# Attention prepared one step earlier, the first MLP's raw weights loaded ahead into their final places, and their low parts on VectorE

## The chip, the cores and the metric

The kernel runs on one core of one Trainium2 chip. The metric is the device time of one execution in microseconds (us). Times are compared between executions on the same chip.

## The reference

Four inputs of attention per batch and head: 512 local and 32 global tokens, 4 batches, 8 heads, head size 64. A local query sees the 32 global keys and the local keys within 32 positions; a global query sees all keys. The result, 2176 rows of 512, goes through two MLPs.

```python
def sm(s):
    e = np.exp(s - np.max(s, axis=-1, keepdims=True))
    return e / (np.sum(e, axis=-1, keepdims=True) + 1e-09)
out_g = np.matmul(sm(scale * q_g @ k_all.T), v_all)              # k_all: global and local keys
s_l = concat([scale * q_l @ k_g.T, where(|i - j| <= 32, scale * q_l @ k_l.T, -1e9)])
out_l = np.matmul(sm(s_l), concat([v_g, v_l]))
x = [out_g, out_l] as rows of 512                                # 2176 x 512
h = x @ moe_w_in;   x = np.maximum(0.01 * h, h) @ moe_w_out      # 512 x 2048, 2048 x 512
h = x @ moe2_w_in;  x = (h - np.tanh(h)) @ moe2_w_out
```

The four weight matrices come as 64-bit floats.

## The kernel before

**Numbers.** Matmuls of the MLPs and of the scores are made of three: each operand is split into a rounded high part and a low part (value minus high part), and high x high, low x high and high x low are added in PSUM. ScalarE writes the high part, VectorE or GpSimd subtracts.

**Weights.** A weight tile is 128 x 512. `load_w` (line 99) brings its 64-bit words (512 KB) into a raw buffer, of which there are two (tag `wraw`). `convert_w` (113) makes 32-bit floats of them: an Abs on ScalarE (119) and four VectorE steps (120, 121, 125, 128), of which the last reads the raw buffer for the last time. `split_w` (133) then writes the high part on ScalarE (134) and subtracts the low part (135), for the first MLP on GpSimd. The 16 tiles of the first layer (`in`) stay in `win_h` and `win_l`; those of the second (`out`) are kept in few buffers and stored to DRAM, from where later chunks fetch them (`wo_fetch`). `w_jobs` (656) lists the conversions in order, in and out in turn; `w_load` issues the next load, `w_job` converts the tile loaded longest ago. The conversion steps may not be put ahead of the last attention output (`issue_after`, 684).

**Attention.** There are 32 units (pairs of heads for half a sequence). The work on unit pp is: `k_prep` and `q_prep` (transposes, then high and low parts, 321, 322, 334, 335), `score` (three matmul groups), `smax_a` (mask and row minimum on VectorE, 374; exponential on ScalarE, 380), `smax_b` (sums, reciprocals, and the normalisation, on GpSimd for units under 16, line 394, else on VectorE, 399), `p_trans` (transposes of the probabilities, two copies on ScalarE, 412), `av` (products with the values, high and low part, 437, 439), `g_score` (the global queries' scores). `stage(pp)` (742) lists, in TensorE's order: score and softmax of pp, keys and queries of pp+1, the transposes and then the value products of pp-1, the global scores of pp. Steps of the global rows (`gtodo`) are put in between.

**Order.** A prologue runs stages 0 to 8 (`PRE`, line 51) and converts three first-layer tiles (`LW`). Then come 80 items of the first MLP, (chunk c, tile f) for five chunks of 512, 512, 512, 256 and 384 rows: `mlp1_a` is the first layer for tile f, `mlp1_b`, two items later (`SKEW`), adds the second layer's product. Beside the items of chunks 0 to 2 run the remaining stages (`beside`, 840), eight beside the 16 items of chunk 0. In chunk 0 each item also converts one `in` and one `out` tile (869 to 872). The second MLP's weights are converted into DRAM beside items 22 to 44 (`w2_job`), then 80 items of the second MLP follow. TensorE's instructions up to item 77 stand in program order by hand (`fix`, 799); on the other engines a planner orders instructions by priority and its own costs; SP issues all DMAs in order.

**PSUM.** The eight banks are `h`, four `y` and three `att` banks; in the prologue the attention uses `att` and `y` in turn, later only the three `att` banks (`tag`, 737).

The functions that the diff touches, and what calls them:

Of the kernel before, what the change touches and what calls it, by code (L numbers as in the profile page):

```python
# [13 lines left out]
I32 = mybir.dt.int32  # L14
# [7 lines left out]
def kernel(  # L22
# [28 lines left out]
    PRE, LW, SKEW = 9, 3, 2  # L51
# [17 lines left out]
    win_h = [persist.tile([128, ND, 128], F32R, name=f"winh{f}") for f in range(NF)]  # L69
    win_l = [persist.tile([128, ND, 128], F32R, name=f"winl{f}") for f in range(NF)]  # L70
# [120 lines left out]
    def mlp1_g(c, f, h):  # L191
# [165 lines left out]
    def norm(pp):  # L357
        return "pool" if pp < 16 else "dve"
# [44 lines left out]
    def p_trans(pp, h, tag):  # L403
# [7 lines left out]
        pt = att.tile([128, 2, 2, 128], F32, tag="pt", name="pt", bufs=4)  # L411
        nc.scalar.activation(pt.rearrange("p j c q -> p (j c q)"), ps, AF.Copy)
# [143 lines left out]
    def w2_place(kind, f, t):  # L556
        if kind == "in":
            split_w(t, flat(win_h[f]), flat(win_l[f]), nc.vector)
# [97 lines left out]
    w_jobs = []  # L656
    for f in range(LW):
        w_jobs.append(("in", f))
    for f in range(NF):
        if f:  # L660
            w_jobs.append(("out", f - 1))
        if f + LW < NF:
            w_jobs.append(("in", f + LW))
    w_jobs.append(("out", NF - 1))
    w_jobs.reverse()
    w_raw = []
# [5 lines left out]


    def w_load():
        if w_jobs:
            kind, f = w_jobs.pop()
            w_raw.append((kind, f, load_w(kind, w1_in if kind == "in" else w1_out, f)))

    def w_job():
        if not w_raw:  # L680
            return
        kind, f, raw = w_raw.pop(0)
        after = anchor[0] if 1 & 2 and anchor[0] is not None else last_av[0] if 1 & 1 else None
        with tc.issue_after(after.ins) if after is not None and nw[0] >= 0 else ExitStack():
            w = convert_w(raw)
        if kind == "in":
            split_w(w, flat(win_h[f]), flat(win_l[f]), nc.gpsimd)
        else:
            wo_split(f, w)
# [6 lines left out]
            later.append(store)  # L696

# [31 lines left out]
    jobs_done = [0]  # L729
# [12 lines left out]
    def stage(pp):  # L742
# [3 lines left out]
        if pp < NU // 2:  # L746
            ops.append(lambda: (score(pp, [tag(), tag()]), smax_a(pp), smax_b(pp)))
        nx = pp + 1
        if nx < NU // 2:
            if pp % 2:  # L750
                ops.append(lambda: load_kq((pp + 3) // 2))
            ops.append(lambda: (k_prep(nx, tag()), q_prep(nx, tag())))
            if nx % (2 * NP) == 0:
                ops.append(lambda: qg_prep(nx // (2 * NP), tag()))
        if pp > 0:
            ops.append(lambda: p_trans(pp - 1, 0, tag()))
            ops.append(lambda: (gtodo.pop(0)() if gtodo else None, p_trans(pp - 1, 1, tag())))

            def values_of():
                av(pp - 1, tag())  # L760
                if pp < NU // 2:
                    g_score(pp, tag())
                if gtodo:
                    gtodo.pop(0)()
                if pp % 2 == 0:
                    load_v((pp + 2) // 2)

            ops.append(values_of)
        else:
            ops.append(lambda: g_score(pp, tag()))  # L770
        hv, p = divmod(pp, NP)
        b, a = divmod(hv, 2)
        if pp < NU // 2 and a == 1 and p % 2 == 1:
            quad = p // 2

            def put():
                gtodo.extend([
                    lambda: (g_load(b, 2 * quad), g_smax(b, quad)),
                    lambda: (g_trans(b, quad, tag()), g_trans2(b, quad, tag())),
                    lambda: (g_av(b, quad, 0, tag()), g_load(b, 2 * quad + 1)),  # L780
                    lambda: g_av(b, quad, 1, tag()),
                ])

            ops.append(put)
# [22 lines left out]
    if True:  # L807
# [8 lines left out]
        w_load()  # L816
        qg_load(0)
        load_v(0)
        load_kq(1)
# [4 lines left out]
        w_load()  # L824
        for pp in range(PRE):
            for op in stage(pp):
                op()
            if pp >= 3 and jobs_done[0] < LW:
                w_job()
                w_load()  # L830
                stores()
                jobs_done[0] += 1
# [131 lines left out]
```

## Time and profile before

| | |
|---|---|
| median of 3 runs | 1006.79 us (1005.72 to 1009.12) |
| profiled execution, own time | 1006.56 us |
| its span, first to last instruction | 1004.8 us |
| TensorE busy, mean granted clock | 939.9 us (94%), 0.971 |
| VectorE, ScalarE, GpSimd busy | 663.6, 544.2, 102.0 us |
| data moved | 127.13 MB, mean 127 GB/s |

All rows are of the one profiled execution, and microseconds count from its first instruction. PE is TensorE's matmul, DVE is VectorE, ACT ScalarE, POOL GpSimd, SP the engine that issues the DMAs. Instructions that follow each other on an engine overlap a little at their ends, so a sum of durations is more than the busy time. A TensorE that is busy may still run at half clock: PEclk is the granted share of 2.4 GHz.

### The profile page before, as it was taken

Reading aid. Unit: us, or ns where it says so; the run is one execution under the profiler, and the core shown is the slowest. Engines: PE = TensorE matmul, PEld = TensorE weight load, DVE = VectorE, ACT = ScalarE, POOL = GpSimd, SP = SyncE. Lnnn points to the kernel's source line nnn. Section 1 sums busy time; section 2 is a strip of 40 time slices with the busy share of each in tenths; the row PEclk is TensorE's granted clock in tenths of the full one; section 3 lists DMA queues with packets and bytes.
Section 4 is the critical chain, followed back from the end, with each engine's and each line's share of the span. In section 5 each row is a group of like instructions: output and inputs, shape, how many; then the busy total and the mean of one; then the engine's idle time right before and its main releaser. Section 6 shows DMA issues by size and latency. Waiting matters only on the chain.

```text
span 1004.8 us, 15724 instructions
## 1 busy us (share of the span) xinstructions
PE 939.9 (94%) x5480; PEld 785.6 (78%) x5480; DVE 663.6 (66%) x1489; ACT 544.2 (54%) x1231; POOL 102.0 (10%) x123
## 2 busy tenths in 40 slices
PE   4877988889999999998999999999999999999998
PEld 3655766667787787786789999888888888899987
DVE  2456978864356675765421333988888888888886
ACT  4566655654555455554532344755554655655565
POOL 3334343421000000000000000000000000000022
PEclk9779999899999999998999999999999999999999
DMA  7345666675547779875565677200200010010010
GB/s 161 87 109 146 192 188 182 178 220 162 152 134 228 224 230 268 249 236 179 157 220 183 192 216 230 95 1 1 74 1 1 21 43 1 1 43 1 1 33 22
DMA packets 144943, 127.13 MB, mean 127 GB/s; under 512 B 89184, under 2 KB 107616, under 8 KB 144864
## 3 DMA queue, kind: packets, MB, share of 16 engines
q1 hardware_dynamic: 144864, 126.13, 42.1%
q8 instruction: 43, 0.70, 0.3%
q14 instruction: 36, 0.29, 0.1%
HBM read 100.40 MB, written 25.69 MB: 125 GB/s over the span
## 4 chain that ended last, share of the span: by engine, by line
PE 65%; DMA 15%; DVE 9%; ACT 6%; issue 2%; SPq 2%; ACTq 0%; DVEq 0%
PE h L55 29%; PE o L55 19%; PE y L55 11%; DMA wraw<-in_moe_w_in_dram 4%; DMA wraw<-in_moe_w_out_dram 3%; DMA w2od<-wf 2%; DMA wf<-w2od 2%; ACT e L380 2%; DVE wf L128 2%; PE avps L55 2%; DVE wt L125 2%; ACT wf L119 2%; PE sps L55 1%; DVE wf L120 1%; PE ptps L410 1%
## 5 line engine op out<-in xcount | busy, mean ns | idle before, releaser
L55 PE MATMUL h<-xh,winh 128*128 128x512 f32 (+2 forms) x640 | 236.3, 369 | 3.1 <-ACT g L196 3.0
L55 PE MATMUL h<-xl,winh 128*128 128x512 f32 (+2 forms) x640 | 231.6, 362 | 0.0
L55 PE MATMUL h<-xh,winl 128*128 128x512 f32 (+2 forms) x640 | 231.5, 362 | 0.0
L55 PEld LDWEIGHTS h<-xh,winh 128*128 128x128 f32 x640 | 122.0, 191 | 20.8 <-ACT g L196 3.9
L55 PEld LDWEIGHTS h<-xl,winh 128*128 128x128 f32 x640 | 121.8, 190 | 16.7
L55 PEld LDWEIGHTS h<-xh,winl 128*128 128x128 f32 x640 | 122.0, 191 | 15.7
L55 PE MATMUL y<-gh,woh 128*128 128x512 f32 (+2 forms) x320 | 123.2, 385 | 0.2 <-ACT yst L225 0.2
L55 PE MATMUL y<-gh,wol 128*128 128x512 f32 (+2 forms) x320 | 116.8, 365 | 0.0
L55 PE MATMUL y<-gl,woh 128*128 128x512 f32 (+2 forms) x320 | 116.5, 367 | 0.0
L55 PE MATMUL o<-wo2h,gh 128*128 128x512 f32 x255 | 100.2, 393 | 0.0
L55 PE MATMUL o<-wo2l,gh 128*128 128x512 f32 x255 | 99.5, 390 | 0.0
L55 PE MATMUL o<-wo2h,gl 128*128 128x512 f32 x255 | 98.2, 392 | 0.0
L592 ACT ACTIVATE u<-h 128x512 f32<-128x512 f32 (+2 forms) x80 | 42.6, 532 | 94.9 <-PE h L55 72.2
L198 DVE TENSOR_TENSOR gl<-g,gh 128x512 fp32r<-128x512 f32 (+2 forms) x80 | 51.7, 646 | 63.6 <-ACT gh L197 63.5
L380 ACT ACTIVATE e<-e,st 128x224 f32<-128x224 f32 (+1 forms) x128 | 58.7, 460 | 34.0 <-DVE st L374 33.6
L119 ACT ACTIVATE wf<-wraw 128x512 f32<-128x512 f32 x64 | 42.6, 666 | 62.8 <-DMA wraw<-in_moe_w_in_dram 21.2
L196 ACT ACTIVATE g<-h 128x512 f32<-128x512 f32 (+2 forms) x80 | 42.2, 527 | 58.0 <-PE h L55 56.8
L618 POOL TENSOR_TENSOR gl<-p,gh 128x256 fp32r<-128x256 f32 x16 | 11.9, 742 | 558.9 <-ACT gh L617 557.0
L55 PEld LDWEIGHTS y<-gl,woh 128*128 128x128 f32 x320 | 61.3, 192 | 8.7
L617 ACT ACTIVATE gh<-p 128x512 fp32r<-128x512 f32 (+2 forms) x80 | 45.5, 568 | 41.1 <-DVE p L601 41.1
L120 DVE TENSOR_SCALAR wf<-wf 128x512 f32<-128x512 f32 x64 | 31.8, 502 | 54.1 <-ACT wf L119 53.9
L55 PEld LDWEIGHTS y<-gh,woh 128*128 128x128 f32 x320 | 61.4, 192 | 7.7 <-ACT yst L225 0.4
(112 smaller groups left out, 1752.6 us busy)
## 6 DMA issues: line engine op xcount, KB each, us to landing
wraw<-in_moe_w_in_dram SPq DMA_DIRECT2D x32, 512.0 KB, 4.6
wraw<-in_moe_w_out_dram SPq DMA_DIRECT2D x32, 512.0 KB, 4.1
woh<-wod SPq DMA_DIRECT2D x64, 256.0 KB, 3.8
wol<-wod SPq DMA_DIRECT2D x64, 256.0 KB, 3.2
qr<-in_q_l_dram SPq DMA_DIRECT2D x32, 128.0 KB, 3.3
vn<-in_v_l_dram SPq DMA_DIRECT2D x32, 128.0 KB, 2.8
wod<-woh SPq DMA_DIRECT2D x16, 256.0 KB, 4.0
wod<-wol SPq DMA_DIRECT2D x16, 256.0 KB, 3.3
```

Of the source, the lines that this page charges most:

```text
L55: nc.tensor.matmul(o, lhsT, rhs, start=start, stop=stop)
L119: nc.scalar.activation(w, hw.bitcast(F32), AF.Abs)
L120: nc.vector.tensor_scalar_max(w, w, TINY)
L125: nc.vector.scalar_tensor_tensor(out=t, in0=hw, scalar=-0x40000000, in1=t, op0=ALU.bitwise_and, op1=ALU.bitwise_or)
L128: nc.vector.scalar_tensor_tensor(out=w.bitcast(I32), in0=lw, scalar=29, in1=t, op0=ALU.logical_shift_right, op1=ALU.bitwise_or)
L196: anchor[0] = nc.scalar.activation(g[:, :N], h[:, :N], AF.Prelu, alpha=0.01)
L198: nc.vector.tensor_sub(gl[:, :N], g[:, :N], f32(gh)[:, :N])
L380: nc.scalar.activation(e[:, h, j, s0 : s0 + n], e[:, h, j, s0 : s0 + n], AF.Exp, bias=st[:, k : k + 1], scale=-1.0, accum_out=st[:, 4 + k ...
L410: nc.tensor.transpose(ps[:, k * 128 : (k + 1) * 128], e[:, h, j, c0 : c0 + 128], ident)
L592: nc.scalar.activation(u, h, AF.Square)
L617: nc.scalar.activation(gh[:, :N], p, AF.Copy)
L618: eng["pool" if i == order2[-1] and [0, 16][0] <= f < [0, 16][1] else "dve"].tensor_sub(gl[:, :N], p, f32(gh)[:, :N])
```

## The change

One more stage runs in the prologue. In a stage, keys and queries of the next unit are now prepared ahead of the unit's score, and the value products of unit s-2 open the stage; the transposes of unit s-1 close it. All 16 raw tiles of the first layer are loaded in the prologue, each into the memory that its two parts take in the end (one tile of 128 x 2 x 512 for both, tag `win{f}`); one conversion follows each stage from the third on, eight in all. The other eight are converted beside items 0 to 7 of chunk 0. Second-layer tiles alone use the two raw buffers, and their next load is issued right behind a conversion. The low parts of all first-MLP weights go to VectorE. GpSimd normalises units 0 to 7 only; for these, the second copy of the transposed probabilities goes from ScalarE to VectorE. The probabilities have two buffers instead of four, the values of the global rows two instead of one. The second MLP's conversions may now not be put ahead of the activation's low part (before: of the activation).

```diff
-    PRE, LW, SKEW = 9, 3, 2
+    PRE, SKEW = 10, 2
+    win_h, win_l = {}, {}
+    def win_tile(f):
+        t = persist.tile([128, 2, DM], F32R, tag=f"win{f}", name=f"win{f}")
+        win_h[f], win_l[f] = [t[:, k].rearrange("p (k n) -> p k n", k=ND) for k in range(2)]
+        return t
...
-    def load_w(kind, w, f):
-        raw = mlp.tile([128, DM, 2], I32, tag="wraw", name="wraw", bufs=2)
+    def load_w(kind, w, f, raw=None):
+        if raw is None:
+            raw = mlp.tile([128, DM, 2], I32, tag="wraw", name="wraw", bufs=2)
...
-        split_w(w, hi, lo, nc.gpsimd)
+        split_w(w, hi, lo, nc.vector)
...
-        anchor[0] = nc.scalar.activation(g[:, :N], h[:, :N], AF.Prelu, alpha=0.01)
+        nc.scalar.activation(g[:, :N], h[:, :N], AF.Prelu, alpha=0.01)
...
-        nc.vector.tensor_sub(gl[:, :N], g[:, :N], f32(gh)[:, :N])
+        anchor[0] = nc.vector.tensor_sub(gl[:, :N], g[:, :N], f32(gh)[:, :N])
...
-        return "pool" if pp < 16 else "dve"
+        return "pool" if pp < 8 else "dve"
...
-        pt = att.tile([128, 2, 2, 128], F32, tag="pt", name="pt", bufs=4)
-        nc.scalar.activation(pt.rearrange("p j c q -> p (j c q)"), ps, AF.Copy)
+        pt = att.tile([128, 2, 2, 128], F32, tag="pt", name="pt", bufs=2)
+        if h and pp < 8:
+            nc.vector.tensor_copy(pt.rearrange("p j c q -> p (j c q)"), ps)
+        else:
+            nc.scalar.activation(pt.rearrange("p j c q -> p (j c q)"), ps, AF.Copy)
...
-        vn = att.tile([128, 4, 2, D], F32, tag="vn", name="vn", bufs=1)
-        vg = att.tile([SG, 2, D], F32, tag="vg", name="vg", bufs=1)
+        vn = att.tile([128, 4, 2, D], F32, tag="vn", name="vn", bufs=2)
+        vg = att.tile([SG, 2, D], F32, tag="vg", name="vg", bufs=2)
...
+    def in_load():
+        if in_todo:
+            f = in_todo.pop(0)
+            place = persist.tile([128, DM, 2], I32, tag=f"win{f}", name=f"inraw{f}")
+            in_raw.append((f, load_w("in", w1_in, f, place)))
+    def converted(raw):
+        with tc.issue_after(last_av[0].ins) if last_av[0] is not None else ExitStack():
+            return convert_w(raw)
+    def in_job():
+        if in_raw:
+            f, raw = in_raw.pop(0)
+            w = converted(raw)
+            t = win_tile(f)
+            split_w(w, t[:, 0], t[:, 1], nc.vector)
+    def out_job():
+        if out_raw:
+            f, raw = out_raw.pop(0)
+            wo_split(f, converted(raw))
...
+            out_load()
...
+        def cols():
+            if s >= 2:
+                av(s - 2, tag())
+                if s % 2:
+                    load_v((s + 1) // 2)
+            if 1 <= s <= last + 1:
+                g_score(s - 1, tag())
...
+        def keys():
+            k_prep(s + 1, tag())
+            q_prep(s + 1, tag())
...
+            if s % 2 == 0:
+                load_kq((s + 4) // 2)
+        if s >= 1:
+            ops.append(cols)
+        if s + 1 <= last:
+            ops.append(keys)
+        if s <= last:
+            ops.append(lambda: (score(s, [tag(), tag()]), smax_a(s), smax_b(s)))
+        if 1 <= s <= last + 1:
+            ops.append(lambda: p_trans(s - 1, 0, tag()))
+            ops.append(lambda: (p_trans(s - 1, 1, tag()), gtodo.pop(0)() if gtodo else None))
...
         for pp in range(PRE):
             for op in stage(pp):
                 op()
-            if pp >= 3 and jobs_done[0] < LW:
-                w_job()
-                w_load()
-                stores()
-                jobs_done[0] += 1
...
+            in_load()
+            in_load()
+            if pp >= 2:
+                in_job()
+            if pp == PRE - 2:
+                out_load()
+                out_load()
...
-            last = (starts[c + 1] + sizes[c + 1]) // HALF * NP if c < 2 else NU // 2
+            last = (starts[c + 1] + sizes[c + 1]) // HALF * NP + 1 if c < 2 else NU // 2 + 1
...
-                    for _ in range((f + LW < NF) + (f > 0)):
-                        w_job()
-                        w_load()
+                    in_job()
+                    if f > 0:
+                        out_job()
```

## Rows read from the trace of the kernel before

**Rows 1.** Windows: busy time and (instructions) of each engine, then clock and DMA
```profile
core 0: us, PE busy (x) PEld busy (x) DVE busy (x) ACT busy (x) POOL busy (x), PEclk, DMA share, GB/s
0.00:90.00 90.00, 61.44 (x468) 48.48 (x468) 43.66 (x164) 50.97 (x157) 31.05 (x53) 0.85 0.50 120
90.00:225.00 135.00, 115.32 (x708) 89.77 (x709) 107.72 (x226) 80.62 (x193) 54.78 (x45) 0.92 0.65 190
225.00:300.00 75.00, 74.38 (x492) 58.93 (x491) 33.18 (x112) 38.73 (x102) 3.44 (x5) 1.00 0.53 152
350.00:400.00 50.00, 48.39 (x315) 37.96 (x313) 30.88 (x87) 26.81 (x68) 0.21 (x1) 1.00 0.83 249
```

**Rows 2.** Line 196, the activation of each item, in 91 to 236 and 241 to 299
```profile
L196 ACT ACTIVATE g<-h x16: 574/586/607, 91.8 to 235.2; 128x512 f32<-128x512 f32 x16
...
L196 ACT ACTIVATE g<-h x8: 573/598/598, 241.3 to 298.2; 128x512 f32<-128x512 f32 x8
```

**Rows 3.** Waits of TensorE, 90 to 225: us in total, times, longest
```profile
PE sps L55 <- DVE xl L439: 4.3, 2, 2.5
...
PE ptps L410 <- DVE kl L322: 2.9, 1, 2.9
```

**Rows 4.** Waits of ScalarE, 90 to 225
```profile
ACT wf L119 <- DMA wraw<-in_moe_w_out_dram: 15.4, 11, 2.8
...
ACT wf L119 <- DMA wraw<-in_moe_w_in_dram: 8.1, 8, 2.4
```

**Rows 5.** Waits of the DMA queue (SP), 90 to 225
```profile
SPq L108 <- DVE wf L128: 46.6, 19, 6.4
```

**Rows 6.** Line 125: ns of one, shortest/median/longest
```profile
L125 DVE SCALAR_TENSOR_TENSOR wt<-wraw,wt x64: 677/691/1726, 44.4 to 476.4; 128x512 int32<-128x512 int32 x64
```

**Rows 7.** Groups by line: count | busy us, mean ns | idle before, us, and its releasers
```profile
L374 DVE CUSTOM_DVE_ANT_0 e<-sps,mask 128x224 f32<-128x224 f32 (+1 forms) x128 | 40.3, 369 | 15.5 <-PE sps L55 15.5
...
L394 POOL TENSOR_TENSOR e<-e,st 128x512 f32<-128x512 f32 x32 | 34.8, 1109 | 50.1 <-ACT pt L412 26.2 <-DVE st L390 21.3 <-PE h L55 2.6
...
L135 POOL TENSOR_TENSOR winl<-wf,winh 128x512 fp32r<-128x512 f32 x16 | 23.4, 1461 | 25.8 <-ACT winh L134 23.8 <-ACT xh L550 1.9
...
L399 DVE TENSOR_SCALAR e<-e,st 128x192 f32<-128x192 f32 (+1 forms) x64 | 16.6, 323 | 0.4
L322 DVE TENSOR_TENSOR kl<-kps,kh 128x352 fp32r<-128x352 f32 x32 | 16.5, 516 | 10.6 <-ACT kh L321 10.6
...
L135 DVE TENSOR_TENSOR wo2l<-wf,wo2h 128x512 fp32r<-128x512 f32 x15 | 10.4, 692 | 24.8 <-ACT wo2h L134 24.6
```

**Rows 8.** Timeline of VectorE: start us, us
```profile
119.12 0.43 DVE L121 TENSOR_SCALAR wt<-wf 128x512 int32<-128x512 int32 x1
119.58 0.69 DVE L125 SCALAR_TENSOR_TENSOR wt<-wraw,wt 128x512 int32<-128x512 int32 x1
120.19 0.35 DVE L374 CUSTOM_DVE_ANT_0 e<-sps,mask 128x192 f32<-128x192 f32 x1
...
120.78 1.20 DVE L198 TENSOR_TENSOR gl<-g,gh 128x512 fp32r<-128x512 f32 x1
```

**Rows 9.** Line 321, one per stage, in 36 to 50, 42 to 79 and 21 to 30
```profile
L321 ACT ACTIVATE kh<-kps x3: 463/463/465, 36.9 to 49.8; 128x352 fp32r<-128x352 f32 x3
...
L321 ACT ACTIVATE kh<-kps x5: 446/463/465, 43.3 to 78.3; 128x352 fp32r<-128x352 f32 x5
...
L321 ACT ACTIVATE kh<-kps x2: 442/442/443, 21.5 to 29.7; 128x352 fp32r<-128x352 f32 x2
```

**Rows 10.** Waits of TensorE, 0 to 90
```profile
PE avps L55 <- ACT pt L412: 18.5, 13, 4.0
```

**Rows 11.** Waits of TensorE, 225 to 530
```profile
PE qps L329 <- DVE st L374: 3.8, 2, 3.6
PE gavps L55 <- DMA vn<-in_v_l_dram: 3.6, 5, 1.5
```

**Rows 12.** Windows of the prologue, columns as in rows 1
```profile
22.00:36.00 14.00, 11.66 (x73) 9.35 (x75) 4.68 (x18) 7.09 (x23) 4.07 (x4) 0.52 0.34 74
...
70.00:94.00 24.00, 17.62 (x181) 13.57 (x181) 16.66 (x57) 16.69 (x52) 10.20 (x12) 1.00 0.48 125
```

More of the change, by code (lines that the diff above doesn't have):

```diff
@@ L67, in bank @@
         return psum.tile([128, 512], F32, tag=tag, name=name)
-    win_h = [persist.tile([128, ND, 128], F32R, name=f"winh{f}") for f in range(NF)]
-    win_l = [persist.tile([128, ND, 128], F32R, name=f"winl{f}") for f in range(NF)]
+    win_h, win_l = {}, {}
[3 more added lines that the diff above has]
+        return t
     xh = [persist.tile([128, ND, n], F32R, name=f"xh{n}") for n in (512, 640)]
@@ L557, in w2_place @@
         if kind == "in":
-            split_w(t, flat(win_h[f]), flat(win_l[f]), nc.vector)
+            d = win_tile(f)
+            split_w(t, d[:, 0], d[:, 1], nc.vector)
         else:
@@ L653, in mlp2_b @@
                         nc.sync.dma_start(out=out[b * S : b * S + SG, :], in_=st[b * SG : (b + 1) * SG, :])
[L656 to L666, printed above, removed]
+    in_raw, out_raw, in_todo, out_todo = [], [], list(range(NF)), list(range(NF))
     later = []
@@ L671, in stores, with out_load @@
             later.pop(0)()
[L674 to L689, printed above, removed]
+    def in_load():
[3 more added lines that the diff above has]
+            in_raw.append((f, load_w("in", w1_in, f, place)))
+    def out_load():
+        if out_todo:
+            f = out_todo.pop(0)
+            out_raw.append((f, load_w("out", w1_out, f)))
+    def converted(raw):
[11 more added lines that the diff above has]
+            wo_split(f, converted(raw))
             hi, lo = wo_t[f]
@@ L728 @@
     gtodo = []
-    jobs_done = [0]
     w2_first = 22
@@ L740, in tag, with stage @@
         return t
-    def stage(pp):
+    def stage(s):
         ops = []
[L746 to L784, printed above, removed]
@@ new lines, in stage @@
+        last = NU // 2 - 1
+        def cols():
[5 more added lines that the diff above has]
+                g_score(s - 1, tag())
+                hv, p = divmod(s - 1, NP)
+                b, a = divmod(hv, 2)
+                if a == 1 and p % 2 == 1:
+                    quad = p // 2
+                    gtodo.extend([
+                        lambda: (g_load(b, 2 * quad), g_smax(b, quad)),
+                        lambda: (g_trans(b, quad, tag()), g_trans2(b, quad, tag())),
+                        lambda: (g_load(b, 2 * quad + 1), g_av(b, quad, 0, tag())),
+                        lambda: g_av(b, quad, 1, tag()),
+                    ])
+            if gtodo:
+                gtodo.pop(0)()
@@ new lines, in keys @@
+        def keys():
+            k_prep(s + 1, tag())
+            q_prep(s + 1, tag())
+            if (s + 1) % (2 * NP) == 0:
+                qg_prep((s + 1) // (2 * NP), tag())
+            if s % 2 == 0:
[9 more added lines that the diff above has]
+            ops.append(lambda: (p_trans(s - 1, 1, tag()), gtodo.pop(0)() if gtodo else None))
@@ L815 @@
         build_masks()
-        w_load()
         qg_load(0)
+        load_kq(1)
         load_v(0)
-        load_kq(1)
+        in_load()
         load_v(1)
@@ L827 @@
                 op()
-            if pp >= 3 and jobs_done[0] < LW:
-                w_job()
-                w_load()
-                stores()
-                jobs_done[0] += 1
-        while jobs_done[0] < LW:
-            w_job()
-            w_load()
-            jobs_done[0] += 1
+            in_load()
+            in_load()
+            if pp >= 2:
[3 more added lines that the diff above has]
+                out_load()
         tags[0] = run_tags
@@ L869 @@
                 if c == 0:
-                    for _ in range((f + LW < NF) + (f > 0)):
-                        w_job()
-                        w_load()
+                    in_job()
+                    if f > 0:
+                        out_job()
                 elif c == 4 and f == 0:
@@ L894 @@
                 if one[2] == NF - 1:
-                    w_job()
+                    out_job()
             while fetches:
```

## The prediction

> **What bounds the kernel now.** I read the windows first, then the waits of TensorE and of ScalarE in the bad stretch, then the pace of the repeated work, and single instructions last. The windows [rows 1] split the run in two. From 225 us on TensorE is the bound: in 225 to 300 it idles 0.6 us of 75 at clock 1.00. Before that it isn't: it idles 28.6 us of 90 in the prologue (clock 0.85), and 19.7 us of 135 in 90 to 225 (clock 0.92, so another 0.08 x 135 = 10.8 us of full speed is not granted). That second stretch is chunk 0 of the first MLP, items 0 to 15, with eight attention stages and the conversion of the weights beside it. Its pace: the sixteen activations of line 196 go from 91.8 to 235.2, 143.4 us for 15 items or 9.56 each; eight items of chunk 1, with as many attention stages per item and no conversions to speak of, take 56.9 us for 7, or 8.1 [rows 2]. At that pace TensorE needs 15 x 8.1 = 122 us (somewhat less, since items 0 and 1 have no second layer beside them): 21 us are to be had there, hardly more.
>
> Who takes them: TensorE's longest waits in 90 to 225 are all for VectorE, four rows of 4.3 us down to 2.9, 13.9 together (the first and the last stand) [rows 3]. VectorE was late for two reasons. ScalarE stood 23.5 us at the head of its queue for a raw weight's DMA [rows 4], and what lies behind (exponentials, copies) stood with it. The DMA was late because SP held it 46.6 us until the last conversion step of an earlier tile gave back one of two raw buffers [rows 5]: 29 conversions go through a ring of two. And VectorE is slowed by GpSimd: the step of line 125 takes 0.69 us in the median and up to 1.73 [rows 6]; the difference, 1.04, is one GpSimd multiplication (L394, 1.11 mean) [rows 7].
>
> **The change, part by part.**
>
> *Raw first weights into their final places, out of the ring.* Thirteen of 29 conversions of chunk 0 lose the wait for a buffer; eight remain there, with raw data long landed, and 16 second-layer tiles keep the ring, one per item instead of two. A buffer then has two items, some 16 us, to come round, where it had one. I take the 23.5 us of ScalarE's waits in chunk 0 as gone; bounds 23.5 and, if the two-deep ring still holds the 16 others, 23.5 x 13/29 = 11. What is late next is VectorE itself, so it has to be summed.
>
> *VectorE's load.* Its instructions start closer together than they last: 119.58 to 120.19 for a 0.69 us step, 120.19 to 120.78 for two mask steps that last 0.37 each, and 0.46 for a 0.43 us one [rows 8]. By starts, a conversion is 2 x 0.45 + 2 x 0.61 = 2.1 us, and with the low part moved from GpSimd (1.46 there, 0.69 on VectorE as the same subtraction runs later for the second MLP) 2.75 us [rows 7, 8]. An attention stage is four mask steps, 4 x 0.31, and three low parts, the longest 0.52 and by starts 0.44: with its two tiny instructions I count 2.6 us, and 3.6 with four normalisations of 0.32, by starts 0.25, which now stand on VectorE from stage 8 instead of 16 [rows 7]. Chunk 0: 24 conversions x 2.75 = 66, eight stages x 3.6 = 29, 16 low parts of the activations x 0.61 = 10, the global rows 3: 108 us. That is what VectorE is busy there now, 107.7 [rows 1]: the same terms for now give 29 x 2.1 + 8 x 2.6 + 10 + 3 = 95, so that collisions with GpSimd cost some 13, and the 12 that are added (24 x 0.61 + 8 x 1.0 - 5 x 2.1) take their place. With 13 conversions less to wait for, the stretch is bound by TensorE again, but tightly: the first eight items hold 15 of the 24 conversions, 41 + 5 + 14 + 2 = 62 us of VectorE against 65 of TensorE. I take 8.7 us an item there, halfway from 8.1 to the old pace less a little, and 8.1 in the second half: 8 x 8.7 + 7 x 8.1 = 126 us, against 143.4. Gain 17; bounds 21 (all of it) and -4 (the last rival below, where all its stalls show in chunk 0).
>
> *The prologue, ten stages instead of nine and eight conversions instead of three.* Undisturbed stages take 6.45 us (36.9 to 49.8 for two), those with conversions 8.75 (43.3 to 78.3 for four) [rows 9]; TensorE waited 18.5 us in 13 places for ScalarE's copies of the transposed probabilities [rows 10]. In the new order the value products still come right behind the transposes, so this wait stays in kind; but of two copies one goes to VectorE, and no conversion that waits for a DMA stands ahead of them: I count half of it gone. Per stage VectorE now has 2.6 + 2.75 + 0.6 (the copy) + 0.4 (global rows) + about 0.6 for collisions with GpSimd's normalisations and stages 8 and 9, some 7 us, and that is the new limit: 7.5 us a stage. The second stage's keys are written at 21.5 now [rows 9]; their loads are issued sooner, so I take 20, the tenth stage's at 20 + 8 x 7.5 = 80, and some 8 us for its score, its transposes and item 0: the first line-196 activation comes at 88, against 91.8. Gain 4; bounds 12 (6.45 us a stage) and -8 (each of the 16 GpSimd multiplications holds one VectorE step up by the 1.04 us of rows 6: 17 us instead of 5, the activation at 100). The loads: 11 more tiles by 90 us are 5.8 MB; at the rate of 350 to 400 (249 GB/s for a share of 0.83, so 300 GB/s full) 19 us more of the 16 engines, on 45 now: a share of 0.73, under what that stretch bears [rows 1]. A key load behind two of these comes 3.5 us later and is asked for two stages ahead, so I cost it at nothing.
>
> Here a rule of the Trainium skill speaks against the prologue: the page SBUF — State Buffer, section Who interferes with whom, says that a VectorE instruction with two SBUF inputs and a GpSimd instruction that reads SBUF exclude each other for a whole instruction. The longest step of line 125 agrees with it; its median says that most steps meet nothing. By the rule the lower bound above would hold whenever a step is queued at each multiplication, and the sum would be 12 us higher, 995.5; by the median it is mine.
>
> *From chunk 1 on.* The named waits of 225 to 530 that this touches are 3.6 us for one buffer of values (now two) and 3.8 for st [rows 11]. The next keys are prepared a step earlier, the probabilities have two buffers instead of four but are read before the next two are written. I take 2 us gained, between 7 (both gone) and -7 (as much put elsewhere). The new anchor of the second weights' conversions, the low part instead of the activation, starts each a little later on a VectorE that is 62% busy (350 to 400) [rows 1]: nothing, since the idle third covers it.
>
> **The sum.** Own time of the profiled execution 1006.56 (span 1004.8), which is the median of the runs, 1006.79, within 0.02%. 1006.6 - 4 - 17 - 2 = **983.5 us**, with 973 to 996 for this case alone.
>
> **Rivals.**
>
> *The prologue runs cold.* In 21.5 to 29.7 one stage took 8.2 us [rows 9] at a granted clock of one half (0.52 in 22 to 36), with TensorE busy 11.7 of 14 us: there the clock, not VectorE, set the pace [rows 12]. TensorE had idled up to 4.0 us at a time before its products [rows 10]. More conversions between the stages give more such pauses. Then the tenth stage's keys come at 20 + 8 x 8.2 = 86, the 8 us behind them become 11, the first activation is at 97, and the prologue loses 5 instead of gaining 4: 992.5. For: 0.85 mean clock now. Against: from 70 to 94 it was 1.00 with three tiles converting [rows 12]. The Trainium skill's page TensorE: Matmul & The Clock Gate, section HAM oscillation, describes such a pattern, where waits between bursts keep bringing the half clock back; by it the whole prologue would run so.
>
> *Nothing is recovered in chunk 0.* TensorE's waits name VectorE, and VectorE is as busy as before; if evictions queue behind conversions as now, the pace stays at 9.56 and the prologue's 4 us are spent on the longer tenth stage: 1006. For: 62 of 65 us in the first half. Against: ScalarE's stalls, which made the bunching, go.
>
> *The low part stalls VectorE (the slow side).* The subtraction needs ScalarE's rounded copy of what VectorE has just written: VectorE, ScalarE, VectorE, in queues that don't overtake. GpSimd took this wait before. Where the same subtraction already stands on VectorE, it idles before it 24.6 us for 15 tiles, 1.64 each [rows 7]. If each of 32 conversions pays 1.64: the first activation at 88 + 13 = 101, chunk 0 at 108 + 24 x 1.64 = 147 us, its last at 248.6 instead of 235.2: 1020. With a stall w the end is 88 + 8w + 108 + 24w, so it is slower from w = 1.2 us on, and below 0.7 the stall is hidden in chunk 0. Against: that row is from the end of the first MLP, where little else was there to fill in.
>
> **How the numbers follow.** Forecast 0.64, cold prologue 0.14, nothing recovered 0.10, stalled low parts 0.12. Below 970 I leave 0.06 (both bounds good), above 1004 some 0.14. A measurement of this kernel tells about 0.3% (3 us) from no change: faster by more 0.78 (first two), within it 0.10, slower 0.12.
>
> **What would show it.** Right: ScalarE's waits for raw DMAs near nothing in chunk 0; line 125 at 0.69 without the 1.7 us outliers there; sixteen line-196 activations within 130 us, the first before 92; VectorE busy about 85% of that stretch; the windows from 300 us on as now. The forecast is wrong if VectorE idles over 1.2 us before each low part (slower), if the half clock fills the prologue, or if the gain of chunk 0 comes back as new waits in 235 to 500.

## The result and the profile after

The changed kernel takes 981.76 us in the median (979.37 to 982.36, 4 runs), against 1007.0 for the kernel before: a ratio of 0.9743 with a 95% interval of 0.972 to 0.9766. The profiled execution took 981.75, its span 980.0. Forecast were 983.5. The time is right; the sum behind it is less so, since one term came out on the other side and two others made up for it.

The windows of the changed kernel, over the stretches of [rows 1] and with the same columns:

```profile
0.00:90.00 90.00, 63.63 (x522) 50.44 (x523) 64.01 (x205) 54.91 (x165) 24.68 (x47) 0.79 0.78 199
90.00:225.00 135.00, 130.28 (x854) 101.75 (x853) 107.69 (x303) 89.74 (x222) 1.81 (x6) 1.00 0.59 173
225.00:300.00 75.00, 70.17 (x445) 55.46 (x443) 35.12 (x106) 35.78 (x91) 0.41 (x2) 0.99 0.54 157
350.00:400.00 50.00, 49.28 (x278) 39.00 (x277) 33.04 (x90) 26.24 (x64) 0.21 (x1) 1.00 0.82 252
```

In 90 to 225 TensorE went from 115 us busy at clock 0.92 to 130 at 1.00, with VectorE as busy as before (10 us of chunk 1 now stand in this window) and GpSimd all but off. The prologue has no such gain: VectorE is busy 64 us there instead of 44, and the clock is lower, 0.79 for 0.85.

The activation of each item, line 204 now (the line answering to [rows 2]), in 93 to 215:

```profile
L204 ACT ACTIVATE g<-h x16: 572/597/607, 93.1 to 214.6; 128x512 f32<-128x512 f32 x16
```

With these marks the span splits into a prologue (to the first activation), chunk 0 (to the sixteenth) and the rest:

| profiled execution | prologue | chunk 0 | rest | span |
|---|---|---|---|---|
| before | 91.8 | 143.4 | 769.6 | 1004.8 |
| forecast gain | 4 | 17 | 2 | 23 |
| after | 93.1 | 121.5 | 765.4 | 980.0 |
| measured gain | -1.3 | 21.9 | 4.2 | 24.8 |

Chunk 0 as a window, first of the kernel before, then of the changed one:

```profile
92.00:235.00 143.00, 125.31 (x775) 97.55 (x776) 112.53 (x242) 84.41 (x203) 54.80 (x46) 0.93 0.65 186
93.00:215.00 122.00, 117.28 (x780) 91.53 (x780) 99.28 (x276) 81.24 (x200) 1.81 (x6) 1.00 0.61 178
```

TensorE idles 4.7 us instead of 17.7, and its busy time for about as many matmuls is 8.0 us shorter, at clock 1.00 instead of 0.93. VectorE is busy 99 us, 81% of the stretch.

Waits of TensorE, of ScalarE and of SP in chunk 0 (93 to 215), to be read beside [rows 3], [rows 4] and [rows 5]:

```profile
PE h L55 <- ACT g L204: 1.9, 1, 1.9
PE y L55 <- DVE wol L143: 1.3, 1, 1.3
PE sps L55 <- DVE kl L330: 0.6, 1, 0.6
```
```profile
ACT wf L127 <- DMA wraw<-in_moe_w_out_dram: 10.0, 5, 6.1
```
```profile
SPq L116 <- DVE wf L136: 20.5, 8, 5.7
```

TensorE's waits for VectorE are down to 2 us. ScalarE still waits 10 us for raw tiles, all of the second layer, and SP 20.5 instead of 46.6; they no longer reach TensorE.

The conversion step and the low parts that the prediction spoke of: line 133 (125 before, [rows 6]) over the whole run, for both kinds of raw buffer, then what VectorE idled ahead of the low parts of chunk 0 (line 143, 93 to 215; us, times):

```profile
L133 DVE SCALAR_TENSOR_TENSOR wt<-wraw,wt x48: 680/692/695, 97.4 to 455.8; 128x512 int32<-128x512 int32 x48
L133 DVE SCALAR_TENSOR_TENSOR wt<-inraw,wt x16: 679/688/694, 22.4 to 141.2; 128x512 int32<-128x512 int32 x16
```
```profile
  ACT woh L142: 1.0, 1
  ACT win L142: 0.6, 1
```

No execution of this step is longer than 0.695 us any more, and 22 low parts idle VectorE 1.6 us in all, 0.07 each instead of the 1.64 of the slow rival.

The prologue: line 329, one per stage (line 321 in [rows 9]), and TensorE's waits in 0 to 93 (of before: [rows 10]):

```profile
L329 ACT ACTIVATE kh<-kps x9: 442/463/467, 13.4 to 83.5; 128x352 fp32r<-128x352 f32 x9
```
```profile
PE avps L55 <- ACT pt L423: 7.5, 5, 4.1
PE gtps L535 <- DVE st L398: 3.9, 1, 3.9
PE gtps L535 <- DVE sg L526: 3.7, 1, 3.7
PE kps L326 <- DMA kr<-in_k_l_dram: 3.6, 1, 3.6
PE avps L55 <- DVE pt L421: 2.5, 2, 1.7
```

Eight stages take 70.1 us, 8.8 each instead of 7.5. They begin at 13.4 instead of the 20 that I took, and the first activation comes 9.6 us behind the last of them instead of 8: -6.6 + 10.1 + 1.6, 5.1 us later than the 88 of the forecast. As a window, and then one stage of it by itself:

```profile
13.40:83.50 70.10, 49.29 (x414) 39.67 (x414) 54.66 (x170) 44.44 (x135) 18.80 (x22) 0.75 0.85 222
63.60:72.60 9.00, 9.00 (x71) 7.80 (x69) 5.68 (x21) 5.72 (x18) 2.57 (x5) 0.50 0.62 139
```

VectorE is busy 54.7 us, 6.8 a stage, so the 7 us that I had summed were about right; but it idles 22% of the time, and the granted clock is 0.75, a mean of stretches at full and at half clock. In the stage from 63.6 TensorE was busy without a break, at half clock.

The waits for copied probabilities fell from 18.5 to 10.0 us (7.5 for ScalarE's copies, 2.5 for those that VectorE makes now), about the half that I had counted, but 7.6 us of new ones stand ahead of the global rows' transposes, which in the new order come half a stage behind their softmax.

### The profile page after: what moved, and what is told of

It is laid out like the page before. It is cut to its first block, busy times and chain, and to the rows that moved or that the text cites. A ratio compares the mean times of both kernels' runs of the same rounds, so it can differ in the third digit from the quotient of the medians.

```text
span 980.0 us, 15683 instructions
## 1 busy us (share of the span) xinstructions
PE 932.2 (95%) x5480; PEld 777.9 (79%) x5480; DVE 673.9 (69%) x1561; ACT 540.6 (55%) x1223; POOL 39.6 (4%) x75
## 3 DMA queue, kind: packets, MB, share of 16 engines
q1 hardware_dynamic: 144864, 126.13, 43.3%
## 4 chain that ended last, share of the span: by engine, by line
PE 63%; DMA 18%; DVE 8%; ACT 5%; SPq 3%; issue 2%; ACTq 0%; DVEq 0%
PE h L55 28%; PE o L55 19%; PE y L55 9%; DMA wf<-w2od 4%; DMA wraw<-in_moe_w_in_dram 4%; DMA wraw<-in_moe_w_out_dram 3%; DMA inraw<-in_moe_w_in_dram 2%; DMA w2id<-wf 2%; PE avps L55 2%; DMA w2od<-wf 2%; PE sps L55 1%; ACT e L388 1%; PE ptps L418 1%; DVE wf L136 1%; DVE wt L133 1%
## 5 line engine op out<-in xcount | busy, mean ns | idle before, releaser
L55 PE MATMUL h<-xh,win 128*128 128x512 f32 (+2 forms) x1280 | 358.9, 364 | 2.9 <-ACT g L204 2.9
L55 PEld LDWEIGHTS h<-xh,win 128*128 128x128 f32 x1280 | 227.1, 188 | 38.4 <-ACT g L204 4.9
L55 PE MATMUL h<-xl,win 128*128 128x512 f32 (+2 forms) x640 | 230.6, 360 | 0.0
L55 PEld LDWEIGHTS h<-xl,win 128*128 128x128 f32 x640 | 120.6, 188 | 17.5
L206 DVE TENSOR_TENSOR gl<-g,gh 128x512 fp32r<-128x512 f32 (+2 forms) x80 | 48.8, 609 | 71.4 <-ACT gh L205 70.7
L604 ACT ACTIVATE u<-h 128x512 f32<-128x512 f32 (+2 forms) x80 | 42.5, 532 | 91.8 <-PE h L55 85.0
L127 ACT ACTIVATE wf<-wraw 128x512 f32<-128x512 f32 x48 | 32.1, 670 | 66.9 <-DMA wraw<-in_moe_w_in_dram 19.5
L55 PEld LDWEIGHTS y<-gh,wol 128*128 128x128 f32 x320 | 60.5, 189 | 7.9 <-DVE wol L143 2.4
L630 DVE TENSOR_TENSOR gl<-p,gh 128x512 fp32r<-128x512 f32 (+1 forms) x64 | 41.9, 654 | 24.2 <-ACT gh L629 24.1
L610 ACT ACTIVATE u<-u,tc_a 128x512 f32<-128x512 f32 (+2 forms) x80 | 52.7, 659 | 6.7 <-DVE p L608 4.2
L55 PEld LDWEIGHTS o<-wo2h,gl 128*128 128x128 f32 x255 | 47.9, 188 | 10.3
```

The lines of the kernel that those rows point to most:

```text
L55: nc.tensor.matmul(o, lhsT, rhs, start=start, stop=stop)
L127: nc.scalar.activation(w, hw.bitcast(F32), AF.Abs)
L206: anchor[0] = nc.vector.tensor_sub(gl[:, :N], g[:, :N], f32(gh)[:, :N])
L604: nc.scalar.activation(u, h, AF.Square)
L610: nc.scalar.activation(u, u, AF.Square, bias=tc_a2)
L630: eng["pool" if i == order2[-1] and [0, 16][0] <= f < [0, 16][1] else "dve"].tensor_sub(gl[:, :N], p, f32(gh)[:, :N])
```

## The experiments

Twelve kernels ran. Ratios are to the kernel before, measured beside each, with 95% intervals. Marks in time come from the one profiled execution of each. Four of these are no good measure of their kernel's time: with three conversions it took 980.44 us (the other runs 972.95 to 973.38), with ordered loads 988.07 (982.42 to 983.49), with old order, three conversions and ordered loads 972.54 (967.34 to 969.42), and with the mixed order at the end 977.89 (980.29 to 982.99).

**Which part made chunk 0 shorter?** Three candidates: the raw tiles out of the ring (A), the low parts off GpSimd (B), the stage order (C). Each is undone alone, and B is done alone. One more part could matter there, the normalisation of units 8 to 15 on VectorE instead of GpSimd; no run undoes it by itself.

Low parts back on GpSimd:

```diff
-        split_w(w, hi, lo, nc.vector)
+        split_w(w, hi, lo, nc.gpsimd)
...
-            split_w(w, t[:, 0], t[:, 1], nc.vector)
+            split_w(w, t[:, 0], t[:, 1], nc.gpsimd)
```

> The changed kernel, but the low parts of the first MLP's weights are subtracted on GpSimd again, all else as changed. Theory A (the gain of chunk 0 is the raw tiles taken out of the ring of two; the low parts on VectorE cost it about what the collisions with GpSimd had cost): VectorE in chunk 0 loses 24 x 0.61 = 15 us and gets some 12 us of collisions back, so 982 us, plus or minus 4, and line 125's counterpart shows 1.5 to 1.7 us outliers again. Theory B (the gain is the end of the collisions): most of the 22 us of chunk 0 goes, 998 to 1003. Theory C (the gain is the new order of a stage): 982, within 3.

986.89 us, ratio 0.979 (0.9746 to 0.9833), between the theories. Its activations, its conversion step, two of ScalarE's waits in chunk 0, and chunk 0 as a window:

```profile
L204 ACT ACTIVATE g<-h x16: 573/588/600, 95.4 to 222.0; 128x512 f32<-128x512 f32 x16
```
```profile
L133 DVE SCALAR_TENSOR_TENSOR wt<-wraw,wt x48: 674/692/1784, 101.5 to 461.5; 128x512 int32<-128x512 int32 x48
```
```profile
ACT wf L127 <- POOL wol L143: 5.1, 5, 2.0
ACT wf L127 <- POOL win L143: 3.0, 5, 1.4
```
```profile
95.00:222.00 127.00, 118.97 (x780) 92.12 (x779) 105.90 (x257) 82.06 (x202) 32.76 (x29) 1.00 0.58 171
```

Chunk 0 takes 126.6 us, 5.1 more. The collisions are back (1784 ns): VectorE, rid of these subtractions, is busy 105.9 us, more than the 99.3 of the changed kernel. And something that I had not counted: the next conversion waits 8.1 us for one of the two `wf` buffers, which GpSimd's slower subtraction holds. The clock is 1.00 with either. How the 5.1 us divide between collisions and buffers is not shown.

The kernel before with nothing but its low parts on VectorE:

```diff
-        split_w(w, hi, lo, nc.gpsimd)
+        split_w(w, hi, lo, nc.vector)
...
-            split_w(w, flat(win_h[f]), flat(win_l[f]), nc.gpsimd)
+            split_w(w, flat(win_h[f]), flat(win_l[f]), nc.vector)
```

> The kernel before, with only the low parts of the first MLP's weights moved from GpSimd to VectorE. Theory A: ScalarE's waits for raw tiles in chunk 0 stay above 15 us, and so does the pace of 9.5 us an item: 1005 us, plus or minus 4. Theory B: the collisions are gone, chunk 0 falls by most of 22 us: 984 to 992. Theory C: 1005, within 3.

996.58 us, ratio 0.989 (0.9855 to 0.9925): 11 us faster, where A had expected nothing and B 15 to 23. Its chunk 0 as a window, to be read beside the one of the kernel before (92 to 235, above):

```profile
90.00:222.50 132.50, 117.98 (x777) 91.04 (x776) 112.76 (x269) 83.94 (x203) 18.78 (x20) 1.00 0.69 204
```

VectorE's busy time (the third number) doesn't move, 112.8 and 112.5: collisions out and subtractions in cancel, as forecast. But the stretch is 10.5 us shorter all the same. TensorE idles 14.5 us instead of 17.7, and its clock is 1.00 instead of 0.93; 0.07 x 143 = 10 us at full speed had not been granted. In busy and idle time of TensorE, the 10.5 us are 7.3 and 3.2. What the conversions did to the clock was no term of my sum. Waits for buffers that GpSimd holds are not the reason here: in 92 to 235 of the kernel before ScalarE has none, and its waits for raw tiles even grow, from 23.1 to 29.2 us. That fewer and shorter hold-ups of VectorE kept the clock up fits, but no run isolates it.

The raw tiles of the first layer through the ring of two again, three converted in the prologue (all else as changed):

```diff
-            in_load()
-            in_load()
-            if pp >= 2:
-                in_job()
+            if pp >= 4 and jobs_done[0] < LW:
+                w_job()
+                w_load()
...
-                    in_job()
-                    if f > 0:
-                        out_job()
+                    for _ in range((f + LW < NF) + (f > 0)):
+                        w_job()
+                        w_load()
```

> The changed kernel, but the first layer's raw tiles go through the ring of two again, in turn with the second layer's, with three converted in the prologue; new stage order, low parts on VectorE. Theory A: chunk 0 is back at 9.3 to 9.8 us an item, 140 to 147 us, while the prologue is some 5 us shorter than changed (five conversions less): 996 to 1004. Theory B and theory C: 980 to 986, since what they name is still there.

987.24 us, ratio 0.9786 (0.9742 to 0.9829). Its activations, and ScalarE's waits in chunk 0:

```profile
L204 ACT ACTIVATE g<-h x16: 569/590/609, 86.7 to 220.7; 128x512 f32<-128x512 f32 x16
```
```profile
ACT wf L127 <- DMA wraw<-in_moe_w_in_dram: 16.0, 6, 5.0
ACT wf L127 <- DMA wraw<-in_moe_w_out_dram: 11.4, 11, 2.2
```

Chunk 0 is 134.0 us, 12.5 longer, with 27.4 us of ScalarE's waits for raw tiles: more than B and C say, and less than the 140 to 147 of A. But the prologue is 6.4 us shorter, without the loads and five of the conversions, so the total is only 5 us worse. That pointed to the prologue.

The old stage order with everything else of the change:

```diff
-    PRE, SKEW = 10, 2
+    PRE, SKEW = 9, 2
...
-    def stage(s):
+    def stage(pp):        # the function of the kernel before
...
-            if pp >= 2:
+            if pp >= 1:
```

> The changed kernel, but with the stage order of before (nine stages in the prologue, keys behind the score, value products right behind their transposes in the same stage); raw tiles loaded ahead, eight converted in the prologue, low parts on VectorE. Theory A: chunk 0 keeps 120 to 127 us; what the order moved elsewhere (the prologue, chunks 1 and 2) is at most 6 us: 980 to 988. Theory B: the same. Theory C: chunk 0 is back at over 135 us: 995 to 1005.

979.22 us, ratio 0.9718 (0.9673 to 0.9762): as the changed kernel, within the intervals. The activations:

```profile
L204 ACT ACTIVATE g<-h x16: 574/593/606, 89.4 to 208.4; 128x512 f32<-128x512 f32 x16
```

Chunk 0 is 119.0 us.

So theory C falls for chunk 0. A is worth 134.0 - 121.5 = 12.5 us there in the new order. In the old one it is 132.6 - 119.0 = 13.6, but this pair also differs in who normalises units 8 to 15 and in buffers. B is worth 5.1 beside A and 10.8 alone. Neither gives the 22 alone: with B undone 143.4 - 126.6 = 16.8 are left, with A undone 143.4 - 134.0 = 9.4.

**What made the prologue long?** Three theories, told in the expectations: loads (L), VectorE's conversions (V), the global rows' steps (G).

One raw load per stage instead of two:

```diff
             in_load()
-            in_load()
...
                     in_job()
+                    in_load()
```

> The changed kernel, with one raw first-layer tile loaded per stage instead of two (eleven in the prologue, five beside items 0 to 4). Asks what ended the prologue at 93.1 us instead of 88. Theory L (the loads: the DMA share was 0.99 in 14 to 50, where 0.73 was forecast as a mean): the share there falls under 0.80, TensorE's waits for key and query loads (5.1 us in all) go, the first activation comes at 87 to 90, total 976 to 979. Theory V (VectorE's conversions set the prologue's pace): first activation at 92 to 95, total 980 to 983. Theory G (the global rows' transposes, which stand half a stage behind their softmax in the new order): the same as V, with the waits of 7.6 us on them still there.

985.18 us, ratio 0.9797 (0.9759 to 0.9834). It did not test L: the loads wait for nothing, and SP issued them as early as before. The 16 issues of this kernel, and of the changed one:

```profile
L116 SPq DMA_DIRECT2D inraw<-in_moe_w_in_dram x16: 411/505/1667, 11.8 to 53.4; - x16
```
```profile
L116 SPq DMA_DIRECT2D inraw<-in_moe_w_in_dram x16: 368/506/1674, 11.8 to 53.9; - x16
```

The window 14 to 50 of this kernel, and of the changed one:

```profile
14.00:50.00 36.00, 22.72 (x186) 17.43 (x186) 28.04 (x86) 22.42 (x68) 11.23 (x12) 0.86 0.98 273
```
```profile
14.00:50.00 36.00, 23.39 (x195) 18.26 (x197) 28.53 (x87) 23.08 (x71) 11.23 (x12) 0.81 0.99 275
```

The same with each load ordered behind the key loads, which wait for their buffers:

```diff
-            in_raw.append((f, load_w("in", w1_in, f, place)))
+            with tc.issue_after(last_kq[0].ins):
+                in_raw.append((f, load_w("in", w1_in, f, place)))
```

> The changed kernel, with one raw first-layer tile loaded per stage instead of two and each load ordered behind the key and query loads of its stage, which wait for their buffers; five tiles are loaded beside items 0 to 4. The run with one load per stage and no such order issued them as early as before (share 0.98 in 14 to 50), so it did not test theory L. Theory L (raw loads in a bunch hold up the prologue): share in 14 to 50 under 0.80, first activation at 87 to 90, total 976 to 979. Theory V (VectorE's eight conversions set the pace): first activation at 92 to 95, total 980 to 984.

983.32 us, ratio 0.9768 (0.9737 to 0.9798), first activation at 95.3: no gain, by the median either.

```profile
L116 SPq DMA_DIRECT2D inraw<-in_moe_w_in_dram x16: 371/506/1196, 11.8 to 99.5; - x16
```
```profile
14.00:50.00 36.00, 25.55 (x194) 20.16 (x192) 28.59 (x88) 22.28 (x67) 11.24 (x12) 0.76 0.94 228
```

The issues now spread to 99.5 us. The rate in 14 to 50 fell by a sixth, the share only to 0.94, not under 0.80, so this weakens L without settling it.

Three conversions in the prologue instead of eight (13 beside items 0 to 12 of chunk 0):

```diff
-            if pp >= 2:
+            if pp >= 7:
                 in_job()
```

> The changed kernel, with three conversions in the prologue instead of eight, and thirteen beside items 0 to 12 of chunk 0; all 16 raw tiles are still loaded in the prologue. Theory V: the five conversions, 14 us of VectorE, leave the prologue: first activation at 86 to 89. Theories L and G: it stays at 91 to 94. In chunk 0 VectorE gets 14 us more, 99 + 14 = 113 of some 125, so by the forecast's sum chunk 0 takes 124 to 130 us instead of 121.5: total 979 to 985 under V, 984 to 990 under L and G.

973.35 us, ratio 0.97 (0.9656 to 0.9745), less than either side expected.

```profile
L204 ACT ACTIVATE g<-h x16: 577/598/602, 90.8 to 209.9; 128x512 f32<-128x512 f32 x16
```

The first activation, at 90.8, is above V's 86 to 89 and just under the 91 to 94 of L and G, but this is the execution of 980.44 us, 7 above the median, so it decides nothing. Chunk 0 is not a microsecond longer for five conversions more: 119.1 us here, 119.5 in the run with ordered loads below. Against the run with the old ring, which has as few conversions in its prologue, this is 14.9 us less: A once more.

The global rows one step per stage:

```diff
-            ops.append(lambda: (p_trans(s - 1, 1, tag()), gtodo.pop(0)() if gtodo else None))
+            ops.append(lambda: p_trans(s - 1, 1, tag()))
```

> The changed kernel, with one step of the global rows per stage instead of two, so that a softmax of global scores has a whole stage before its transposes. Theory G: TensorE's two waits of 7.6 us together ahead of these transposes in the prologue go, with some of the half clock behind them: first activation at 86 to 89, total 975 to 978. Theories L and V: the time is waited for elsewhere, first activation at 92 to 95, total 980 to 983.

995.81 us, ratio 0.9899 (0.9852 to 0.9945), the slowest variant of the changed kernel. The first activation stays at 93.2, so G falls. TensorE's waits in 0 to 93:

```profile
PE avps L55 <- ACT pt L423: 17.5, 9, 4.2
PE avps L55 <- DVE pt L421: 5.3, 4, 1.7
```

The 7.6 us at the global transposes went, and 10.0 + 2.8 us more stood at the value products: a wait that only filled time in which the copies were late anyway. Behind chunk 0 it lost 15 us (chunk 2 alone took 133.0 against 122.0); why so much is open.

Then the combinations. Three conversions with one ordered load per stage, in the new order:

```diff
-            if pp >= 2:
+            if pp >= 7:
                 in_job()
...
+            with tc.issue_after(last_kq[0].ins):
```

> The same ordered loads, and three conversions in the prologue instead of eight. Theory L: most of the loss is in the loads, so first activation at 86 to 89, within 2 us of the run with ordered loads alone. Theory V: three conversions alone gave 90.8 and 973 to 980; with the loads ordered nothing is added: first activation at 90 to 92. Both causes, each with its part: 84 to 87, total 970 to 975.

970.77 us, ratio 0.9635 (0.9608 to 0.9661).

```profile
L204 ACT ACTIVATE g<-h x16: 578/599/610, 83.4 to 202.9; 128x512 f32<-128x512 f32 x16
```

With ordered loads, then, five conversions less bring the first activation from 95.3 to 83.4 and the ratio from 0.9768 to 0.9635, well clear of the intervals: V holds. A part of the loads is not clearly shown: beside eight conversions ordering them did nothing, and beside three the mark falls by 7 us, but from the 90.8 that stands for little; by the ratios, 0.97 and 0.9635, it is some 6 us of 1007 with intervals that just overlap.

The old order with three conversions, without and with ordered loads:

```diff
+    def stage(pp):        # the function of the kernel before, PRE = 9
...
-            if pp >= 2:
+            if pp >= 6:
                 in_job()
```

> The old stage order (nine stages in the prologue) with raw tiles loaded ahead, low parts on VectorE, and three conversions in the prologue instead of eight. The old order alone gave 979, three conversions alone 973 to 980; if the two add, first activation at 86 to 88, chunk 0 at 118 to 122, total 973 to 977; if both only remove the same crowd of VectorE work from the prologue, 978 to 981.

> All three: old stage order, three conversions in the prologue, ordered loads of one tile per stage. Theory L: first activation at 84 to 87, total 970 to 975, the best of the runs. Theory V: as without the ordered loads, within 2 us.

971.3 us, ratio 0.9638 (0.9608 to 0.9668), and 968.52 us, ratio 0.9612 (0.9582 to 0.9641); first activations at 77.3 and 78.7. Stages, activations and chunk 0 of the former:

```profile
L329 ACT ACTIVATE kh<-kps x9: 442/464/467, 11.7 to 65.1; 128x352 fp32r<-128x352 f32 x9
```
```profile
L204 ACT ACTIVATE g<-h x16: 577/598/602, 77.3 to 198.2; 128x512 f32<-128x512 f32 x16
```
```profile
77.00:198.00 121.00, 116.08 (x775) 89.87 (x775) 112.77 (x303) 87.46 (x206) 1.74 (x6) 1.00 0.60 173
```

A stage takes 6.7 us. In the old order, eight conversions against three: 89.4 - 77.3 = 12.1 us of prologue for five conversions, which are 5 x 2.75 = 14 us of VectorE. The two prologues as windows, first with eight conversions, then with three:

```profile
0.00:89.40 89.40, 62.52 (x468) 49.91 (x468) 61.97 (x201) 51.97 (x161) 24.78 (x47) 0.83 0.76 194
```
```profile
0.00:77.30 77.30, 55.77 (x468) 44.62 (x468) 47.68 (x173) 45.79 (x149) 23.55 (x47) 0.91 0.89 221
```

TensorE has the same 468 matmuls. Of the 12.1 us it idles 5.3, and 6.8 are its longer busy time at a clock of 0.83 instead of 0.91: more than half of what the conversions cost there comes with the half clock. The prologue with three is the shorter one although its DMA share is higher, 0.89 for 0.76.

Chunk 0 carries the five at 113 of 121 us busy and is 2 us longer. Beside this the loads are a small matter here, the two intervals overlap. The last of these kernels has the lowest median of all, 13 us under the changed one; with its interval it is not told from the two kernels before it.

**Where does the rest come from?** The old order up to unit 25, the new one behind it:

```diff
+    LAST_OLD = 25
+    def stage(s):
+        return stage_old(s) if s <= LAST_OLD else stage_new(s, s == LAST_OLD + 1)
```

> The old stage order up to unit 25 (prologue, chunks 0 and 1) and the new one behind it, all else as changed. The stage order by itself was worth +3 us in total, but unevenly: against the old order it cost 3.7 us in the prologue, 2.4 in chunk 0 and 2.6 in chunk 1 and gave back 7.0 in chunk 2. If chunk 2's gain belongs to the order of its own stages, this kernel keeps both: chunk 2 at 121 to 124 us, total 970 to 974. If it is owed to what was done earlier (work moved ahead into the prologue), chunk 2 stays at 128 to 131 and the total at 977 to 981.

981.02 us, ratio 0.9757 (0.9721 to 0.9793); chunk 2 at 127.4, so its gain under the new order (129.0 to 122.0) is mostly not the order of its own stages. What it is stays open.

## Why the prediction was right, and where it was not

- **Raw tiles out of the ring: right.** Forecast as the main gain, measured at 12.5 to 14.9 us in chunk 0. ScalarE's waits did not go to nothing, as I had taken: of 23.5 us 13.5 went, near the bound of 11, and 10.0 stayed; they are hidden.
- **VectorE's load in chunk 0: too high, and its meaning not right.** That some 13 us of collisions go and about as much work comes was confirmed for the low parts alone, by 112.5 against 112.8. In the changed kernel VectorE is busy 99 us there, not 108; one reason is that 22 conversions stand in the stretch, not 24. But I made of the sum that the move of the low parts gains nothing. It gains 5 to 11 us: beside A with collisions and held buffers gone, alone with a clock that stayed at 1.00.
- **The pace in chunk 0.** The first eight items took 58.6 us instead of 8 x 8.7 = 70, the last seven 62.9 instead of 7 x 8.1 = 57. The crowded half was not the slow one. VectorE at 93% of chunk 0 (old order, three conversions) cost TensorE 2 us at most. So 17 was sized too small; 21.9 is the whole of what TensorE's pace left.
- **The prologue: wrong, -1.3 for 4.** The step that failed is "that is the new limit: 7.5 us a stage". VectorE's work was sized about right, 6.8 us a stage for 7, but it didn't set the pace: a stage took 8.8. The direction, that more conversions there lengthen it, was right (77.3 against 89.4 us in the old order). But the sum gave them VectorE's time alone, and not the waits and the half clock of TensorE, which is what the two windows show. The start at 20 was 6.6 us too late, which hid more than half of the error; in the old order with the same early loads it is 18.0, so that most of this is the new place of the keys, ahead of the score. The reading behind the pace was loose too: the stage from 43.3 to 49.8 stands in both groups of [rows 9], and line 125 starts at 44.4, 51.8 and 59.4 and then only at 84.8, so that the stages from 61.4 to 78.3, of 9.3 and 7.6 us, had no such step of a conversion in them. That loads cost nothing was wrong in the share: 0.73 as a mean was forecast, it was 0.99 in 14 to 50; what that alone cost is not settled.
- **The cold prologue: in part, and more than its chance of 0.14 says.** Its clock is 0.80 over 93 us against 0.85 over 92, 18.6 us of full speed not granted instead of 13.8. In the stage from 63.6 to 72.6 the clock set the pace, as the rival says; in the other seven TensorE idled too. In the prologue of 77.3 us it is 0.91. The Trainium skill (TensorE: Matmul & The Clock Gate, HAM oscillation) has the pattern of waits between bursts that bring the half clock back; this trace agrees for parts of the prologue, 0.50 in that stage, and not for all of it, 0.80.
- **The rule on shared ports.** By it (the Trainium skill, SBUF — State Buffer, Who interferes with whom) the prologue's collisions could cost 17 us; I took 5. No step of line 133, which has two inputs in SBUF, was held in the prologue. Of the low parts, which have two as well, one was (1328 ns). Line 143 in 0 to 93, then line 128 in 0 to 90 and in 90 to 225:

```profile
L143 DVE TENSOR_TENSOR win<-wf,win x9: 673/685/1328, 26.6 to 91.6; 128x512 fp32r<-128x512 f32 x9
```
```profile
L128 DVE TENSOR_SCALAR wf<-wf x9: 417/653/1176, 21.2 to 81.6; 128x512 f32<-128x512 f32 x9
...
L128 DVE TENSOR_SCALAR wf<-wf x23: 407/419/504, 91.3 to 213.4; 128x512 f32<-128x512 f32 x23
```

Some 0.23 us more in the median for nine instructions of line 128, 2 us in all. Six of them were long, each while a multiplication of line 402 ran on GpSimd; the three of 417 to 420 ns met none. Line 128 has one input, so these six are not what the prediction quotes of the rule. Few instructions met, and with the low part it comes to some 3 us.

- **Nothing recovered in chunk 0: fell.** The pace is 8.1 us an item, not 9.56.
- **The stalled low part: fell**, 0.07 us each, where up to 0.7 would have been hidden in chunk 0 and 1.2 was the break-even.
- **From chunk 1 on:** 4.2 for 2, but as a sum of -4.3 in chunk 1, +10.1 in chunk 2, +0.5 in chunks 3 and 4 and -2.1 behind the last activation of the first MLP. This was in the bounds and not understood.

The total came within 2 us since chunk 0 gave 5 more, the prologue 5 less and the rest 2 more than forecast. That the two errors of 5 us cancel is luck.

## What to carry to other kernels

Look where work is moved to, not only where it leaves: the conversions taken out of a stretch in which VectorE had room for them were put into a chain of small dependent steps, and five of them cost 12 us there and 2 us at most in chunk 0. A stage in such a chain is not as long as the work of its busiest engine: here 6.8 us of VectorE made a stage of 8.8, with waits and with half clock behind them. An operation that is moved to another engine at equal busy time can still gain; the gain here was 11 us with VectorE's busy time unchanged, so a sum of busy times alone would not have found it. And a load without a dependency was issued by 54 us whether one or two stood in each stage of the program; ordered behind loads that wait, the same loads spread to 99.5.

## What the runs showed that I had not expected

- In chunk 0 of the kernel before, 10 us of full TensorE speed were lost to half clock, and moving the small subtractions of the first MLP's weights to another engine brought the clock from 0.93 to 1.00 with TensorE's idle time only 3 us less.
- VectorE was busy 113 of 121 us beside a TensorE that kept its pace of 8 us an item.
- The second MLP, which the change does not touch but for its first weights' two parts standing in one tile, takes between 378.4 and 379.6 us from its first tanh to the end in the twelve profiles with that tile, and 377.0 to 377.7 in the two without. No run isolates it.
